# In the first tile, a step's second layer is issued behind the next step's first layer, and the planner's durations are replaced

## The chip, the cores and the metric

The kernel runs on one core of a Trainium2 chip. Its time is the device time of one execution in microseconds (us). Three runs of the kernel before took 511.29, 515.15 and 515.39 us (median 515.15). One more execution was profiled; it took 513.02 us and is the one that the trace describes.

The engines are named as the profile names them: PE (matrix multiply; PEld is its weight load), DVE (vector), ACT (activation functions and copies), POOL (GpSimd) and SP, which here only issues the DMA transfers. Each engine takes its instructions in the order in which they were written, so an instruction that waits holds up everything behind it on its engine.

## The reference

A linear recurrence over 768 positions for each of 4 x 8 heads, and on its 3072 x 384 output a two-layer network with a GELU between:

```python
for t in range(S):                                  # S = 768, D = 48
    cur = einsum('bhd,bhe->bhde', u * k[t], v[t])
    y[t] = einsum('bhd,bhde->bhe', r[t], state + cur)
    state = w * state + einsum('bhd,bhe->bhde', k[t], v[t])
h = x @ w_in                                        # 3072x384 @ 384x2048
g = 0.5 * h * (1.0 + erf(h / sqrt(2)))
return g @ w_out                                    # 3072x2048 @ 2048x384
```

## The kernel before

**The work.** The 768 positions are cut into 6 chunks of 128; with 4 batches, a chunk is a *tile* of 512 tokens for the network. In each chunk the heads are handled as four *groups* (pairs of heads and their time halves): decays are multiplied into the transposed inputs (`T`, `Tb`, line 374) and the keys (`N`, `Nb`, line 380); `scores`, `own`, `gains`, `old`, `new` and `gaps` (lines 402 to 447) are PE products; `keep` (lines 478 and 479) copies a group's output from PSUM (`Y`) into the network's input `xx`, a rounded high part on ACT and the remainder on DVE; every group goes through the one `Y`.

**The network.** A tile has 16 *steps*, one for each 128 hidden units; 6 tiles make 96 steps, `m` = 0 to 95. Every product of 32-bit numbers is three products of rounded parts: high x high, low weight x high, high weight x low. Step m's *first layer* is `product1` (line 553): 9 matmuls of 128 x 512 into the single PSUM bank `Hp`. ACT then applies the GELU twice (`gh`, line 581, the rounded result; `gf`, line 582, the full one) and DVE forms the remainder `gl` (line 583). Step m's *second layer* is `product2` (line 594): 3 matmuls with `gh` and the high weight, 3 with `gh` and the low one, 3 with `gl`, into three banks `O`. `gh` and `gl` are double buffered.

**The weights** come from HBM as 64-bit floats, 768 KB a step, into one of three buffers `raw` (line 316). They are split once, during the first tile, into `wh` and `wl`, which stay in SBUF: per step, ACT runs lines 329 (`wa`), 331 (`wb`) and 339 (`wh`), and DVE runs 333, 335, 337 and 341 (`wl`). A new transfer into a `raw` buffer needs line 331 and 335 of the step that used it; a new `wa` needs line 341 of the step three before.

**What sets the order.** Nothing is written out by hand. `Plan.add` collects every operation with its engine, a duration in ns, a due time, and the names it reads and writes. `Plan.run` plays this list through: it keeps a clock for each engine, always takes the operation that can start first, and between several that are ready the one with the earliest due time (passed back from its users through the durations); the instructions are issued in the order so found. A transfer's end is worked out with a bus of 360 bytes per ns. While PE would idle before the first layer of step 0, `Plan.run` puts in extra matmuls on zeros (`heat`, the "filler"). So a changed duration changes no instruction, but it can change the order on every engine, the number of these fillers, and nothing else.

**Opening.** The loads of the first four groups, two later groups and the first weights are issued in the order of `LOADS` (line 40); `in_turn` lets only three be under way, through a small POOL copy (line 214) that reads a landed buffer and writes a word of the next one. `first_group` handles the four groups of chunk 0; the last three of them are the input that step 0 needs. Here the four are called group 1 to 4, in the order in which they run.

Of the kernel before, what the change touches and what calls it, by code (L numbers as in the profile page):

```python
# [13 lines left out]
AF = mybir.ActivationFunctionType  # L14
# [4 lines left out]
B, H, S, D = 4, 8, 768, 48  # L19
# [7 lines left out]
NJ = DF // 128  # L27
# [5 lines left out]
WMIN, WMAX = 0.7, 1.25  # L33
NT = 8
NEAR = 8
LATER = 10 ** 7
FIRST, STEP, STEP_LAST = 23000, 8400, 3900
WEIGHT_AHEAD, GROUP_AHEAD, GROUP_DUE = 12500, 28000, 20000
# [6 lines left out]
class Plan:  # L45
# [9 lines left out]
    def add(self, eng, ns, at, fn, r=(), w=()):  # L55
        n = len(self.ops)
        deps = set()
        for x in r:
            deps.add(self.writer.get(x))
            self.readers.setdefault(x, []).append(n)  # L60
        for x in w:
            deps.add(self.writer.get(x))
            deps.update(self.readers.pop(x, ()))
            self.writer[x] = n
        deps -= {None, n}
        self.ops.append((eng, ns, at, fn, deps))
        self.reads.append(set(r))
# [3 lines left out]

    def time(self, n):
        e, ns = self.ops[n][:2]
        return 2200 + ns / 360.0 if e == "sp" else ns

    def lag(self, n, m):
        e = self.ops[n][0]
# [4 lines left out]
    def run(self):  # L82
        left = [len(o[4]) for o in self.ops]
        users = [[] for _ in self.ops]
        due = [o[2] for o in self.ops]
        for n in reversed(range(len(self.ops))):
            for d in self.ops[n][4]:
                users[d].append(n)
                due[d] = min(due[d], due[n] - self.time(d) - self.lag(d, n))
        ready_at = [0.0] * len(self.ops)  # L90
        pools = {e: [] for e in self.LAG}
        free = {e: 650.0 for e in self.LAG}
        bus, clear, unread = 0.0, 0.0, 0
        for n, k in enumerate(left):
            if not k:
                pools[self.ops[n][0]].append(n)
        for _ in self.ops:
            best = None
            for e, pool in pools.items():
                if not pool:  # L100
                    continue
                start = max(free[e], min(ready_at[n] for n in pool))
                n = min((n for n in pool if ready_at[n] <= start), key=lambda n: (due[n], n))
                if best is None or start < best[0]:
                    best = (start, e, n)
            start, e, n = best
            if e == "pe" and self.filler:
                fill, buf, ns, room = self.filler
                while not unread and not self.hold and max(free[e], clear) + room < start:
                    fill()  # L110
                    free[e] = max(free[e], clear) + ns
            pools[e].remove(n)
            _, ns, _, fn, _ = self.ops[n]
            if e == "sp":
                free[e] = start + 640
                bus = max(bus, start + 1050) + ns / 360.0
                end = bus + 940
            else:
                free[e] = end = start + ns
            fn()  # L120
            if self.filler:
                unread += sum(self.filler[1] in self.reads[m] for m in users[n] if self.ops[n][0] == "pe")
                if self.filler[1] in self.reads[n]:
                    unread -= 1
                    clear = end + self.LAG[e]
            for m in users[n]:
                ready_at[m] = max(ready_at[m], end + self.lag(n, m))
                left[m] -= 1
                if not left[m]:
                    pools[self.ops[m][0]].append(m)  # L130


def rwkv_gelu_mlp(tc, rkT, rkv, wuT, uN, wmlp, r, k, vT, w, u, out):
    nc = tc.nc
    with ExitStack() as ctx:
# [18 lines left out]
        O = []  # L154
# [4 lines left out]
        wh = [sb([128, 2, DM], F32R, f"wh{j}", cst) for j in range(NEAR)]  # L159
        wl = [sb([128, 2, DM], F32R, f"wl{j}", cst) for j in range(NEAR)]  # L160
# [33 lines left out]
        act = lambda n: 95 + n / 1.2  # L194
        sdve = lambda n: 145 + n / 0.96
        sdve2 = lambda n: 145 + n / 1.92
        sact = lambda n: 225 + n / 1.2
        pool = lambda n: 110 + n * 2.15

        flat2 = lambda x: x.rearrange("p a b c -> p (a b c)")  # L200
# [349 lines left out]
        def product1(x, j, n, ks=range(3), start=False, stop=False):  # L550
            wt, a = ((wh, 0), (wl, 0), (wh, 1))[n]
            for k_ in ks:
                nc.tensor.matmul(O[3], lhsT=wt[j][:, 0, k_ * 128:(k_ + 1) * 128], rhs=x[:, a, k_, :],  # L553
                                 start=start and k_ == ks[0], stop=stop and k_ == ks[-1])
# [8 lines left out]
        def moe1(m, at):  # L563
            t, j = divmod(m, NJ)
            high, low, GH, GL = hidden(m)
            x, X = xx[t % 2], f"xx{t % 2}"

            xr = lambda a, ks=range(3): [f"{X}{k_}{a}" for k_ in ks]
            gaps = [f"{X}{k_}g{i}" for k_ in range(3) for i in range(2)]
            n1 = 2 * j  # L570
            if m == 0:
                gaps0 = lambda k_: gaps[2 * k_:2 * k_ + 2]
                for k_ in range(3):
                    add("pe", 3 * 216, at + k_, lambda k_=k_: [setattr(plan, "filler", None)] + [
                        product1(x, j, n, (k_,), k_ == 0 and n == 0, k_ == 2 and n == 2) for n in range(3)],
                        r=["wh0", "wl0"] + xr("h", (k_,)) + xr("l", (k_,)) + gaps0(k_), w=["H"])
            else:
                for n in range(3):
                    add("pe", 3 * 216, at + n, lambda n=n: product1(x, j, n, start=n == 0, stop=n == 2),
                        r=[f"{('wh', 'wl', 'wh')[n]}{n1}"] + xr("hhl"[n]) + gaps, w=["H"])  # L580
            add("act", 480, LATER, lambda: nc.scalar.activation(out=high, in_=O[3], func=AF.Gelu), r=["H"], w=[GH])  # L581
            add("act", 480, LATER, lambda: nc.scalar.activation(out=gf, in_=O[3], func=AF.Gelu), r=["H"], w=["gf"])  # L582
            add("dve", dve(512), LATER, lambda: nc.vector.tensor_tensor(  # L583
                out=low, in0=gf, in1=high.bitcast(F32), op=ALU.subtract), r=["gf", GH], w=[GL])


# [4 lines left out]
        def product2(j, high, low, n, part):  # L591
            wt, gt = ((wh, high), (wl, high), (wh, low))[n]
            d, dst, a, b = part
            nc.tensor.matmul(bank(dst)[:, a:b], lhsT=wt[j][:, 1, d * 128:(d + 1) * 128], rhs=gt[:, a:b],  # L594
                             start=(j == 0 and n == 0), stop=(j == NJ - 1 and n == 2))

        def moe2(m, at, dest):
# [4 lines left out]
            def go(m, n, which, at):  # L602
                j = m % NJ
                high, low, GH, GL = hidden(m)
                add("pe", 216 * len(which), at, lambda: [product2(j, high, low, n, parts[i]) for i in which],
                    r=[f"{('wh', 'wl', 'wh')[n]}{2 * j + 1}", (GH, GH, GL)[n]], w=[banks[i] for i in which])


            if m < NSTEP - 2:
# [234 lines left out]
```

## Time and profile before

| what | value |
|---|---|
| three runs | 511.29, 515.15, 515.39 us |
| the profiled execution | 513.02 us |
| its span, first to last instruction | 511.2 us |
| PE busy | 484.0 us (95% of the span) |
| DVE, ACT, POOL busy | 242.8, 205.6, 72.2 us |
| granted TensorE clock, mean over the span | 0.975 |
| bytes moved | 43.85 MB, mean 86 GB/s |

The span is read from the first instruction; all times below are from there. A row of the time line has the start in us, the length in us, the engine, the line of the kernel, the operation, `out<-in` by the program's names, the shapes and the count; the bracket gives how long the engine had stood idle and what it waited for. A row of the windows has a stretch of time and in it each engine's busy time (and count), the granted clock of the matrix engine as a fraction, the share of time for which the DMA engines were busy, and GB/s. In the stream of instructions matmuls overlap: three of 128 x 512 take 0.70 us from start to start, though each is shown with about 0.4 us.

### The profile page before, as it was taken

To read this page: it belongs to the slowest core of one execution; us is meant where nothing else is said; L and a number is where in the kernel's file an instruction comes from. 1 tells how busy PE (TensorE), PEld (TensorE's weight loads), DVE (VectorE), ACT (ScalarE), POOL (GpSimd) and SP (SyncE) were. 2 spreads that over 40 slices of the span, in tenths; PEclk is the share of its full clock that TensorE was granted. 3 is DMA by queue.
4 is the path that set the end of the run, shared out by engine and by line. 5 is a ranking of instruction groups with operands and counts; after the bars stand their busy time and mean duration, and the time that the engine had idled before them with its cause. 6 is when DMAs were issued, how large, how long until landed. Compare 5 with 4: busy or idle time off the path is not lost.

```text
span 511.2 us, 11447 instructions
## 1 busy us (share of the span) xinstructions
PE 484.0 (95%) x5006; PEld 387.4 (76%) x5006; DVE 242.8 (47%) x366; ACT 205.6 (40%) x435; POOL 72.2 (14%) x80
## 2 busy tenths in 40 slices
PE   6949998899999999999999999999999999999995
PEld 4846776667787787787787788787787787888884
DVE  5769899899524253724254254253243231211111
ACT  3447567574543433442432432432432422322221
POOL 4310001030220221310220220220220200000000
PEclk9578999999999999999999999999999999999999
DMA  7864528443303033403033123033123000100001
GB/s 221 248 207 170 173 90 263 131 149 94 115 33 94 1 94 94 146 0 94 1 95 93 63 85 92 3 94 93 63 83 92 2 13 10 63 0 1 0 1 66
DMA packets 13190, 43.85 MB, mean 86 GB/s; under 512 B 1808, under 2 KB 2192, under 8 KB 13136
## 3 DMA queue, kind: packets, MB, share of 16 engines
q1 hardware_dynamic: 13136, 43.07, 27.4%
q8 instruction: 41, 0.67, 0.5%
q14 instruction: 13, 0.11, 0.1%
HBM read 36.38 MB, written 4.72 MB: 80 GB/s over the span
## 4 chain that ended last, share of the span: by engine, by line
PE 84%; DMA 9%; DVE 2%; ACT 2%; issue 2%; POOL 1%; SPq 0%; ACTq 0%; POOLq 0%
PE Hp L553 37%; PE O L594 37%; DMA raw<-in_wmlp_dram 7%; PE Y L436 3%; PE Y L426 3%; PE A L407 2%; DMA N<-in_rkv_dram 2%; PE Y L418 1%; PE Y L594 1%; ACT gh L581 1%; DVE wl L341 0%; ACT wh L339 0%; DVE gl L583 0%; ACT wa L329 0%; DVE wa L337 0%
## 5 line engine op out<-in xcount | busy, mean ns | idle before, releaser
L553 PE MATMUL Hp<-xx,wh 128*128 128x512 f32 x576 | 167.6, 399 | 1.4 <-ACT wh L339 1.4
L583 DVE TENSOR_TENSOR gl<-gf,gh 128x512 fp32r<-128x512 f32 x95 | 70.6, 743 | 188.9 <-ACT gf L582 188.8
L581 ACT ACTIVATE gh<-Hp 128x512 fp32r<-128x512 f32 x95 | 56.8, 598 | 232.8 <-PE Hp L553 232.8
L553 PEld LDWEIGHTS Hp<-xx,wh 128*128 128x128 f32 x576 | 107.7, 190 | 26.6 <-ACT wh L339 2.0
L594 PE MATMUL O<-gh,wh 128*128 128x512 f32 (+1 forms) x285 | 83.4, 399 | 5.4 <-ACT gh L581 5.3
L553 PE MATMUL Hp<-xx,wl 128*128 128x512 f32 x288 | 84.4, 400 | 0.2 <-DVE wl L341 0.2
L594 PE MATMUL O<-gl,wh 128*128 128x512 f32 (+1 forms) x285 | 80.8, 390 | 0.1
L594 PE MATMUL O<-gh,wl 128*128 128x512 f32 (+1 forms) x285 | 80.7, 390 | 0.0
L594 PEld LDWEIGHTS O<-gh,wh 128*128 128x128 f32 x285 | 51.6, 188 | 21.9 <-ACT gh L581 10.1
L553 PEld LDWEIGHTS Hp<-xx,wl 128*128 128x128 f32 x288 | 54.3, 189 | 14.0 <-DVE wl L341 1.0
L594 PEld LDWEIGHTS O<-gl,wh 128*128 128x128 f32 x285 | 52.5, 188 | 12.2 <-DVE gl L583 0.6
L594 PEld LDWEIGHTS O<-gh,wl 128*128 128x128 f32 x285 | 52.5, 188 | 11.6
L582 ACT ACTIVATE gf<-Hp 128x512 f32<-128x512 f32 x96 | 56.9, 592 | 0.0
L378 POOL TENSOR_TENSOR Nb<-Nb 128x384 f32<-128x384 f32 x16 | 18.4, 1150 | 256.7 <-DMA Nb<-in_rkv_dram 218.4
L398 ACT ACTIVATE Am<-diag,cs 128x64 f32<-128x64 f32 x128 | 33.5, 344 | 6.3 <-DVE cs L393 6.2
L380 POOL TENSOR_TENSOR Nb<-Nb,WN 128x384 f32<-128x384 f32 x20 | 27.1, 1354 | 51.2 <-DMA Nb<-in_rkv_dram 49.9
L374 DVE TENSOR_TENSOR Tb<-Tb,E 112x1024 f32<-112x1024 f32 x20 | 25.5, 1275 | 5.1 <-DMA Tb<-in_rkT_dram 4.3
L459 DVE SCALAR_TENSOR_TENSOR Sb<-Sa,E,Y 48x192 f32<-48x192 f32 x40 | 16.5, 413 | 14.5 <-ACT xx L478 9.1
L393 DVE TENSOR_REDUCE cs<-Nb 128x8 f32<-128x384 f32 x16 | 8.8, 551 | 28.5 <-POOL Nb L390 28.5
L329 ACT ACTIVATE wa<-raw 128x768 f32<-128x768 f32 x16 | 14.6, 912 | 15.1 <-DMA raw<-in_wmlp_dram 10.2
L478 ACT CAST xx<-Y 112x512 fp32r<-112x512 f32 (+1 forms) x18 | 10.6, 587 | 24.0 <-PE Y L418 19.4
L341 DVE TENSOR_TENSOR wl<-wa,wh 128x768 fp32r<-128x768 f32 x16 | 16.3, 1020 | 2.0 <-ACT wh L339 1.8
(122 smaller groups left out, 393.3 us busy)
## 6 DMA issues: line engine op xcount, KB each, us to landing
raw<-in_wmlp_dram SPq DMA_DIRECT2D x16, 768.0 KB, 4.8
Nb<-in_rkv_dram SPq DMA_DIRECT2D x16, 576.0 KB, 5.4
Tb<-in_rkT_dram SPq DMA_DIRECT2D x20, 448.0 KB, 3.8
out_dram<-raw SPq DMA_DIRECT2D x5, 768.0 KB, 3.6
xx<-x SPq DMA_DIRECT2D x30, 64.0 KB, 3.0
T<-in_rkT_dram SPq DMA_DIRECT2D x4, 448.0 KB, 5.7
N<-in_rkv_dram SPq DMA_DIRECT2D x4, 384.0 KB, 4.7
Nb<-in_rkv_dram SPq DMA_DIRECT2D x4, 384.0 KB, 6.5
```

What stands on the lines that cost most here:

```text
L341: add("dve", sdve(n), LATER, lambda: nc.vector.tensor_tensor(out=both(wl), in0=af, in1=both(wh).bitcast(F32), op=ALU.subtract), r=[A_, f"w ...
L374: add("dve", sdve(1024), LATER, lambda: nc.vector.tensor_tensor(out=flat, in0=flat, in1=E[:, 0, g.p].rearrange("l h i -> l (h i)").unsquee ...
L378: add("pool", pool(DM), LATER, lambda: nc.gpsimd.tensor_tensor(out=g.n[:, 0], in0=g.n[:, 0], in1=g.n[:, 1], op=ALU.mult), r=[g.K], w=[g.R])
L380: add("pool", pool(DM), LATER, lambda: nc.gpsimd.tensor_tensor(out=g.kn, in0=g.kn, in1=WN[:, g.p].rearrange("s j d -> s (j d)").unsqueeze( ...
L398: add("act", sact(HALF) + 60, LATER, lambda x=x, b=b: nc.scalar.activation(out=g.am[:, x, b, :], in_=diag2, func=AF.Copy, scale=g.sums[:, ...
L426: nc.tensor.matmul(g.y[quarter(j), h, b * HALF:(b + 1) * HALF], lhsT=g.s[h][l, b, :], rhs=g.t[l, 0, b, times(h)], start=(b == 0 and not sp ...
L459: add("dve", 420, at, lambda l=l, x=x, more=more: nc.vector.scalar_tensor_tensor(out=g.s[h + 1][quarter(1 - x)], in0=g.s[h][l], scalar=E[l ...
L553: nc.tensor.matmul(O[3], lhsT=wt[j][:, 0, k_ * 128:(k_ + 1) * 128], rhs=x[:, a, k_, :], start=start and k_ == ks[0], stop=stop and k_ == k ...
L581: add("act", 480, LATER, lambda: nc.scalar.activation(out=high, in_=O[3], func=AF.Gelu), r=["H"], w=[GH])
L582: add("act", 480, LATER, lambda: nc.scalar.activation(out=gf, in_=O[3], func=AF.Gelu), r=["H"], w=["gf"])
L583: add("dve", dve(512), LATER, lambda: nc.vector.tensor_tensor(out=low, in0=gf, in1=high.bitcast(F32), op=ALU.subtract), r=["gf", GH], w=[GL])
L594: nc.tensor.matmul(bank(dst)[:, a:b], lhsT=wt[j][:, 1, d * 128:(d + 1) * 128], rhs=gt[:, a:b], start=(j == 0 and n == 0), stop=(j == NJ - ...
```

## The change

Two things. First, every first-layer operation of step m also writes a name `first{m}`, and in steps 0 to 15 (`m < NJ`, the first tile) every second-layer operation of step m also reads `first{m+1}`. The planner therefore places all of step m's second layer behind all of step m+1's first layer. No instruction is added by that: the name stands for no buffer. Second, numbers in the plan are others: the bus goes from 360 to 270 bytes per ns, a matmul from 216 to 234 ns, a GELU from 480 to 600 ns, `gl` from 598 to 678 ns, the splitting and copying operations of ACT by 25 ns more.

```diff
+RATE = 270.0
-        return 2200 + ns / 360.0 if e == "sp" else ns
+        return 2200 + ns / RATE if e == "sp" else ns
-                bus = max(bus, start + 1050) + ns / 360.0
+                bus = max(bus, start + 1050) + ns / RATE
-        sact = lambda n: 225 + n / 1.2
+        sact = lambda n: 250 + n / 1.2
+            first = [f"first{m}"]
-                    add("pe", 3 * 216, at + n, lambda n=n: product1(x, j, n, start=n == 0, stop=n == 2),
-                        r=[f"{('wh', 'wl', 'wh')[n]}{n1}"] + xr("hhl"[n]) + gaps, w=["H"])
-            add("act", 480, LATER, lambda: nc.scalar.activation(out=high, in_=O[3], func=AF.Gelu), r=["H"], w=[GH])
+                    add("pe", 3 * 234, at + n, lambda n=n: product1(x, j, n, start=n == 0, stop=n == 2),
+                        r=[f"{('wh', 'wl', 'wh')[n]}{n1}"] + xr("hhl"[n]) + gaps, w=["H"] + first)
+            add("act", 600, LATER, lambda: nc.scalar.activation(out=high, in_=O[3], func=AF.Gelu), r=["H"], w=[GH])
...
-            add("dve", dve(512), LATER, lambda: nc.vector.tensor_tensor(
+            add("dve", sdve(512), LATER, lambda: nc.vector.tensor_tensor(
...
-                add("pe", 216 * len(which), at, lambda: [product2(j, high, low, n, parts[i]) for i in which],
-                    r=[f"{('wh', 'wl', 'wh')[n]}{2 * j + 1}", (GH, GH, GL)[n]], w=[banks[i] for i in which])
+
+                next_ = [f"first{m + 1}"] if m < NJ else []
+                add("pe", 234 * len(which), at, lambda: [product2(j, high, low, n, parts[i]) for i in which],
+                    r=next_ + [f"{('wh', 'wl', 'wh')[n]}{2 * j + 1}", (GH, GH, GL)[n]], w=[banks[i] for i in which])
```

What it does to the order is shown at three places. **PE in the first tile, around step 5**, before (`wh4` and `wl4` are step 4's weights, `gh0` and `gl0` its hidden values, `gh1` those of step 5):

```order
L553 MATMUL Hp_593<-xx0_120,wh4_79 128x512 x3
L594 MATMUL O0_590<-gl1_126,wh3_78 128x512
L594 MATMUL O1_591<-gl1_126,wh3_78 128x512
L594 MATMUL O2_592<-gl1_126,wh3_78 128x512
L594 MATMUL O0_590<-gh0_123,wh4_79 128x512
L594 MATMUL O1_591<-gh0_123,wh4_79 128x512
L594 MATMUL O2_592<-gh0_123,wh4_79 128x512
L553 MATMUL Hp_593<-xx0_120,wh5_80 128x512 x3
L553 MATMUL Hp_593<-xx0_120,wl5_88 128x512 x3
L553 MATMUL Hp_593<-xx0_120,wh5_80 128x512 x3
L594 MATMUL O0_590<-gh0_123,wl4_87 128x512
```

and after:

```order
L596 MATMUL O0_563<-gl1_126,wh3_78 128x512
L596 MATMUL O1_564<-gl1_126,wh3_78 128x512
L596 MATMUL O2_565<-gl1_126,wh3_78 128x512
L554 MATMUL Hp_566<-xx0_120,wh5_80 128x512 x3
L554 MATMUL Hp_566<-xx0_120,wl5_88 128x512 x3
L554 MATMUL Hp_566<-xx0_120,wh5_80 128x512 x3
L596 MATMUL O0_563<-gh0_123,wh4_79 128x512
L596 MATMUL O1_564<-gh0_123,wh4_79 128x512
L596 MATMUL O2_565<-gh0_123,wh4_79 128x512
L596 MATMUL O0_563<-gh0_123,wl4_87 128x512
```

Before, three matmuls of step 4's second layer stood ahead of step 5's first layer; now all nine stand behind it, and all nine of step 3's second layer lie between the first layers of steps 4 and 5. In the later tiles PE's order is the old one, but for a few groups' products that stand one or two steps earlier or later.

**ACT in the opening**, from the read of `raw1` (step 1's weights) on; `KB1` are group 4's factors, `xx0` are the copies of groups 2, 3 and 4 out of `Y`, `raw2` and the `raw0` behind it the weights of steps 2 and 3. Before:

```order
L329 ACTIVATE wa1_132<-raw1_129 128x768
L386 ACTIVATE KB1_109<-T3_105,uw_100 112x4x64
L478 CAST xx0_120<-Y_68 128x2x4x64
L386 ACTIVATE KB1_109<-T3_105,uw_100 112x4x64
L456 COPY Sb_97<-UE_73 48x192 x2
L331 ACTIVATE wb1_135<-raw1_129 128x768
L329 ACTIVATE wa2_133<-raw2_130 128x768
L478 CAST xx0_120<-Y_68 128x2x4x64
L456 COPY Sb_97<-UE_73 48x192 x2
L478 CAST xx0_120<-Y_68 128x2x4x64
L339 CAST wh0_75<-wa0_131 128x768
```

After:

```order
L330 ACTIVATE wa1_132<-raw1_129 128x768
L332 ACTIVATE wb1_135<-raw1_129 128x768
L479 CAST xx0_120<-Y_68 128x2x4x64
L457 COPY Sb_97<-UE_73 48x192 x2
L340 CAST wh0_75<-wa0_131 128x768
L330 ACTIVATE wa0_131<-raw0_128 128x768
L479 CAST xx0_120<-Y_68 128x2x4x64
L330 ACTIVATE wa2_133<-raw2_130 128x768
L332 ACTIVATE wb0_134<-raw2_130 128x768
L387 ACTIVATE KB0_108<-Tb0_106,uw_100 112x4x64 x2
L340 CAST wh1_76<-wa1_132 128x768
L583 ACTIVATE gh0_123<-Hp_566 128x512
```

The read of `raw2`, which stood ahead of group 3's copy, now stands behind group 4's; `wh0` has moved ahead of group 4's copy, and so has the read of step 3's weights. The first copy into `xx0` and the two `KB1` now stand ahead of the read of `raw1`.

**SP in the opening**, before:

```order
L221 DMA Tb0_106<-in_rkT_dram 112x1024
L224 DMA Nb0_114<-in_rkv_dram 128x768
L316 DMA raw2_130<-in_wmlp_dram 128x1536
L221 DMA Tb1_107<-in_rkT_dram 112x1024
L224 DMA Nb1_115<-in_rkv_dram 128x768
L709 DMA u_sb_91<-in_uN_dram 64x384 x2
L316 DMA raw0_128<-in_wmlp_dram 128x1536
```

and after:

```order
L222 DMA Tb0_106<-in_rkT_dram 112x1024
L225 DMA Nb0_114<-in_rkv_dram 128x768
L317 DMA raw0_128<-in_wmlp_dram 128x1536
L317 DMA raw2_130<-in_wmlp_dram 128x1536
L222 DMA Tb1_107<-in_rkT_dram 112x1024
L225 DMA Nb1_115<-in_rkv_dram 128x768
L713 DMA u_sb_91<-in_uN_dram 64x384
```

The weights of step 3 (the second use of `raw0`) are now issued ahead of those of step 2. At the very start SP issues `T0` ahead of the small table of decays `wu_sb`, which was first before. On POOL one small copy that lets group 3's `N2` be issued now stands ahead of the multiplication of `N0`. PE runs four filler matmuls instead of one ahead of the transpose of the decays (line 305). DVE forms `wl0` ahead of group 4's remainder instead of behind it, and interleaves its work in the first tile differently by one or two instructions at some twenty places.

More of the change, by code (lines that the diff above doesn't have):

```diff
@@ L573, in moe1 @@
                 for k_ in range(3):
-                    add("pe", 3 * 216, at + k_, lambda k_=k_: [setattr(plan, "filler", None)] + [
+                    add("pe", 3 * 234, at + k_, lambda k_=k_: [setattr(plan, "filler", None)] + [
                         product1(x, j, n, (k_,), k_ == 0 and n == 0, k_ == 2 and n == 2) for n in range(3)],
-                        r=["wh0", "wl0"] + xr("h", (k_,)) + xr("l", (k_,)) + gaps0(k_), w=["H"])
+                        r=["wh0", "wl0"] + xr("h", (k_,)) + xr("l", (k_,)) + gaps0(k_), w=["H"] + first)
             else:
                 for n in range(3):
-                    add("pe", 3 * 216, at + n, lambda n=n: product1(x, j, n, start=n == 0, stop=n == 2),
-                        r=[f"{('wh', 'wl', 'wh')[n]}{n1}"] + xr("hhl"[n]) + gaps, w=["H"])
-            add("act", 480, LATER, lambda: nc.scalar.activation(out=high, in_=O[3], func=AF.Gelu), r=["H"], w=[GH])
-            add("act", 480, LATER, lambda: nc.scalar.activation(out=gf, in_=O[3], func=AF.Gelu), r=["H"], w=["gf"])
-            add("dve", dve(512), LATER, lambda: nc.vector.tensor_tensor(
+                    add("pe", 3 * 234, at + n, lambda n=n: product1(x, j, n, start=n == 0, stop=n == 2),
+                        r=[f"{('wh', 'wl', 'wh')[n]}{n1}"] + xr("hhl"[n]) + gaps, w=["H"] + first)
+            add("act", 600, LATER, lambda: nc.scalar.activation(out=high, in_=O[3], func=AF.Gelu), r=["H"], w=[GH])
+            add("act", 600, LATER, lambda: nc.scalar.activation(out=gf, in_=O[3], func=AF.Gelu), r=["H"], w=["gf"])
+            add("dve", sdve(512), LATER, lambda: nc.vector.tensor_tensor(
                 out=low, in0=gf, in1=high.bitcast(F32), op=ALU.subtract), r=["gf", GH], w=[GL])
```

## The prediction

> **What bounds the kernel now.** I read the page's slices first, then the windows, cut at the turns of the program.
>
> ```profile
> PE   6949998899999999999999999999999999999995
> PEclk9578999999999999999999999999999999999999
> ```
> ```profile
> 29.10:33.40 4.30, 0.01 (x2) 0.00 (x0) 1.27 (x3) 2.10 (x4) 0.56 (x3) 0.85 0.47 122
> 33.40:38.28 4.88, 3.35 (x53) 2.70 (x53) 3.96 (x7) 1.37 (x3) 0.80 (x1) 0.50 0.72 208
> 50.70:125.80 75.10, 69.56 (x849) 52.92 (x848) 68.72 (x96) 47.75 (x77) 6.43 (x5) 1.00 0.47 153
> 132.80:511.20 378.40, 370.59 (x3402) 299.78 (x3401) 132.51 (x204) 130.69 (x307) 49.99 (x42) 1.00 0.19 57
> ```
>
> The first number behind the length is PE's busy time, the third DVE's, then ACT's and POOL's; the third from the end is the granted clock. From 132.8 us on PE is busy 370.6 of 378.4 us, DVE a third of that: there matmuls alone bound the kernel, none is added or taken away, and their order is nearly the old one. What the change does, it does ahead of that, in two stages. In the opening (to 38.3 us, the first matmul of step 0) PE waits. In the first tile PE and DVE are both at nine tenths: DVE is busy 68.7 of 75.1 us, because it splits the weights beside its other work.
>
> The opening's largest gap, in the chain of waits (start, length, what) and in the time lines of ACT and PE:
>
> ```profile
> 23.91 7.20 DMA raw<-in_wmlp_dram
> ...
> 32.04 0.59 ACT xx L478
> ...
> 32.66 0.70 DVE xx L479
> ...
> 33.41 1.22 PE Y L446 x4
> ...
> 35.74 1.15 PE Y L436 x32
> ...
> 39.27 3.55 PE Hp L553 x8
> ```
> ```profile
> 26.59 0.90 ACT L331 ACTIVATE wb<-raw 128x768 int32<-128x768 uint32 x1
> 31.13 0.89 ACT L329 ACTIVATE wa<-raw 128x768 f32<-128x768 f32 x1 [3.64 <-DMA raw<-in_wmlp_dram]
> ```
> ```profile
> 26.67 0.75 PE L446 MATMUL Y<-x,spread 112*128 112x256 f32 x4
> ...
> 28.09 0.67 PE L436 MATMUL Y<-Am,N 64*48 64x64 f32 x32
> ```
>
> Group 3's output was ready at 28.09 + 0.67 = 28.76, but its copy began at 32.04: ACT stood at `wa2`, waiting for step 2's weights, with the copy queued behind it. PE idled 4.3 us, the granted clock fell to 0.50, and group 4's products then took 36.89 - 33.41 = 3.5 us where group 3's took 28.76 - 26.67 = 2.1.
>
> **Part 1, the opening.** In the new order `wa2` stands behind both copies. Group 3's copy can start at 28.8 (`wb1` ends at 27.5), 3.25 us earlier, so group 4's products start at 33.41 - 3.25 = 30.15. PE's gap shrinks to about one us, so I take the higher clock to stay: 2.1 us, output ready at 32.25 instead of 36.89.
>
> What is late next is a new wait: group 4's copy stands behind the read of step 3's weights (`raw0`), a transfer that is now issued ahead of step 2's, once line 335 of step 0 has freed the buffer. That operation (0.95 us) now follows this one of line 333 at once:
>
> ```profile
> 21.81 0.55 DVE L333 TENSOR_SCALAR wa<-wa 128x768 int32<-128x768 int32 x1
> ```
>
> So `raw0` is issued at 21.81 + 0.55 + 0.95 = 23.3, nearly when `raw2` was (23.91); with `raw2`'s 7.2 us it lands at 30.5. Longer is possible, since more is under way; the longest landing of such a transfer in the chain is
>
> ```profile
> 100.38 10.45 DMA raw<-in_wmlp_dram
> ```
>
> and would make it 33.75. I take 31. The read (0.9) ends at 31.9, ahead of the output at 32.25; the copy's remainder on DVE, behind `wl0` and three operations more, is done by about 34.5, and step 0's first layer ends at 35 instead of 39.27 + 3.55 = 42.8.
>
> Next `raw2` is late: 786 KB more ahead of it cost 2.8 us at the 280 GB/s of a full queue,
>
> ```profile
> 10.00:20.00 10.00, 8.29 (x243) 7.49 (x244) 7.35 (x11) 5.27 (x11) 5.12 (x9) 0.58 0.94 280
> ```
>
> so it lands at 31.1 + 2.8 = 33.9. Behind it on ACT stand `wa2`, `wb0`, two `KB0`, `wh1` and two GELUs of step 0 that free the bank. From start to start such operations take
>
> ```profile
> 44.62 0.91 ACT L329 ACTIVATE wa<-raw 128x768 f32<-128x768 f32 x1
> 45.41 0.91 ACT L386 ACTIVATE KB<-Tb,uw 112x256 f32<-112x256 f32 x2
> 46.60 0.60 ACT L581 ACTIVATE gh<-Hp 128x512 fp32r<-128x512 f32 x1 [0.28 <-PE Hp L553]
> 47.09 0.59 ACT L582 ACTIVATE gf<-Hp 128x512 f32<-128x512 f32 x1
> 47.57 0.83 ACT L339 CAST wh<-wa 128x768 fp32r<-128x768 f32 x1
> 48.29 0.94 ACT L331 ACTIVATE wb<-raw 128x768 int32<-128x768 uint32 x1
> ```
>
> 0.8 (`wa`, and so I take `wb` and the pair of `KB`), 0.7 (`wh`) and 1.1 (both GELUs): 4.2 us. Step 1's first layer starts at 38.1 and ends, with 2.1 us for nine matmuls, at 40.2. In the chain of before:
>
> ```profile
> 44.46 2.10 PE Hp L553 x9
> 46.56 1.40 PE O L594 x6
> 47.96 1.09 PE A L407 x64
> 49.05 0.36 PE Y L418 x32
> ```
>
> it ended at 46.56, with three matmuls of second layer done (0.7), but without group 5's products (1.09 + 0.36 = 1.45), which the new order has ahead. Like for like the lead is 46.56 + 1.45 - 0.7 - 40.2 = 7.1. Up to `wl2`, with which the window of 50.7 begins, DVE has seven operations of 0.4 to 0.9 us that wait for nothing else late; I take **6.5 us** there.
>
> Bounds: if both transfers take 10.45 us (3 us more than I took) and the clock halves again (1.4 us more for group 4), the lead is about 2.5; if both land in `raw2`'s 7.2, it is 8.5.
>
> Smaller edits. The table `wu_sb` is issued behind `T0`:
>
> ```profile
> 2.69 0.17 DVE L282 TENSOR_SCALAR E<-wu_sb 112x8 f32<-112x8 f32 x1 [0.39 <-DMA wu_sb<-in_wuT_dram]
> 5.88 0.17 POOL L214 COPY N<-T 1x1 f32<-1x1 f32 x1 [3.11 <-DMA T<-in_rkT_dram]
> 9.03 2.00 DVE L374 TENSOR_TENSOR T<-T,E 112x1024 f32<-112x1024 f32 x1 [1.63 <-POOL T L214]
> 13.37 0.92 ACT L329 ACTIVATE wa<-raw 128x768 f32<-128x768 f32 x1 [1.40 <-DMA raw<-in_wmlp_dram]
> ```
>
> At worst it lands with `T0`, at 5.88 less the half us by which `T0` is issued earlier, and the decays come 2.7 us later. DVE idled 1.63 us ahead of `T1`, and ACT then 1.40 for step 0's weights: this cover takes up all but 0.8 us (without it, 2.7). At best it costs nothing, which I take. [...] Three more fillers (0.23 us each) cost 0.4 at most, or nothing if the decays are late. POOL's earlier copy issues `N2` about 1 us sooner, into a full queue; I count nothing.
>
> **Part 2, the first tile.** Waits of the stretch from 50.7 to 132.8, and DVE's group of the split weights:
>
> ```profile
> PE O L594 <- ACT gh L581: 4.6, 8, 0.7
> DVE gl L583 <- ACT gf L582: 1.4, 3, 0.8
> ```
> ```profile
> L341 DVE TENSOR_TENSOR wl<-wa,wh 128x768 fp32r<-128x768 f32 x13 | 13.5, 1036 | 1.9 <-ACT wh L339 1.8
> ```
>
> Eight times PE waits for the GELU of the step whose first layer it has just done. In the new order nine matmuls of the step before (2.1 us) lie there, and the two GELUs need 1.1: these 4.6 us go. What is late next is `wl`: PE can't use a weight that isn't split, and DVE has 68.7 us of work in 75.1. So the tile gains what DVE gains: at least nothing, at most its 6.4 idle us. The waits for a late GELU, or for a cast queued behind one (1.4 + 1.8 = 3.2), should mostly go: I take **3 us**.
>
> Against it: step 15's first layer now needs `wl15` one second layer earlier.
>
> ```profile
> 124.83 0.96 DVE L341 TENSOR_TENSOR wl<-wa,wh 128x768 fp32r<-128x768 f32 x1
> ```
> ```profile
> 131.96 0.87 PE L594 MATMUL O<-gl,wh 128*128 128x512 f32 x3
> ```
>
> Before, 132.8 - 125.8 = 7.0 us passed from `wl15` to the end of step 15's second layer. Now six matmuls of step 15 come, step 14's second layer, step 16's first, step 15's second: 1.4 + 3 x 2.1 = 7.7. With DVE the bound, that costs **0.7 us**.
>
> **Sum.** -6.5 - 3 + 0.7 = -8.8 us. The profiled execution took 513.02 (1.8 outside its span); 513.0 - 8.8 = 504.2, that is 504. The three runs lie from 511.3 to 515.4 around the profiled one, so I forecast against it, not against the median 515.15, with 2 us each way for that scatter.
>
> **Rivals.**
> *The tile is full on both engines* (0.25): DVE's waits nearly all go and the opening gives 8: 8 + 6 - 0.7 = 13.3, 500 us. For it: with the rows' durations few operations of the new order wait long. Against: the present order lost 6.4 us on DVE.
> *The clock falls again* (0.10): PE waits from 35 to 38.1 for `raw2` and ACT. In the windows, 0.85 on average over 4.3 us means that the clock halved 3.0 us after PE fell idle, at 32.1, and came back only at about 42. Steps 1 and 2 then lose 2.1 to 4 us: 506 to 508. [...]
> *The opening's gain is eaten* (0.15): both transfers take 10.45 us; ACT's blocked copy has only changed its place. 2.5 + 0 to 2 - 0.7 leaves 1.8 to 3.8: 509 to 511, within 1%.
> *A ring of waits, slower* (0.05): `wl` of step m lets its first layer run (1.4), then two GELUs (1.1), `wh` of m+1 behind them on ACT (0.75), `wl` of m+1 (0.9); with the second layers queued behind, PE can't fill the time. That is 4.2 us against DVE's 68.7 / 13 = 5.3 a step, so it doesn't bind; it decides once it exceeds 5.3, as it may where a group's products (1.45 and more) lie in it. The largest wait for `wh` is
>
> ```profile
> 62.50 1.43 DVE L341 TENSOR_TENSOR wl<-wa,wh 128x768 fp32r<-128x768 f32 x1 [0.84 <-ACT wh L339]
> ```
>
> If each of 14 steps paid 0.84, 11.8 - 1.8 = 10 us are added; with the opening's low end -2.5 + 10 + 0.7 = +8, 521 us.
>
> **How the numbers follow.** The forecast has the other 0.45. A measurement can't tell less than about 1% (5 us) from no change. Faster by more: forecast, fuller tile, fallen clock, 0.80; within: 0.15; slower: 0.05. The range goes from the fuller tile less scatter, 498.5, to the eaten gain, 510.5.
>
> **What would show it.** PE's 4.3 us idle ahead of group 4 gone; step 0's first layer beginning near 32 instead of 38; the windows of 32 to 42 at clock 1.00; hardly any wait of PE for `gh` ahead of 130, some for `wl` instead; the last split weight near 117 instead of 125.8, and all behind it shifted as a whole. Wrong, if ACT waits for `raw` again ahead of a copy into `xx`, or if DVE's idle time in the tile grows.

## The result and the profile after

| kernel | runs (us) | median | profiled execution | its span, clock |
|---|---|---|---|---|
| before | 511.29, 515.15, 515.39 | 515.15 | 513.02 | 511.2, 0.975 |
| changed | 506.47, 507.28, 509.41 | 507.28 | 509.41 | 507.7, 0.971 |

The ratio is 0.9898 with a 95% interval of 0.986 to 0.9937: faster, by 1.0%. (The medians in the table lie 7.9 us apart, but two of the three runs before lie at the upper end of its longer series.) Nine runs of the changed kernel beside 28 of the one before, in another session (`e4_changed_again` below), gave medians of 507.83 and 512.55, ratio 0.9915 [0.9881, 0.9948]. So the change is worth some 4.5 to 5 us, where 8.8 were forecast. That 507.28 lies in the range of 498.5 to 510.5 says little: the range holds gains from 2.5 to 14.5 us.

The slices of the changed kernel's page (40 equal slices, busy tenths of PE, and the clock that it was granted):

```profile
PE   7879899999999999999999999999999999999995
PEclk9568999999999999999999999999999999999999
```

And its windows, cut where those of before were cut (PE busy, PEld, DVE, ACT, POOL; the third number from the end is the clock, then DMA share and GB/s):

```profile
29.10:33.40 4.30, 2.28 (x50) 1.77 (x53) 1.49 (x3) 0.00 (x0) 0.35 (x2) 0.72 0.70 203
33.40:38.28 4.88, 4.00 (x93) 3.40 (x85) 3.88 (x6) 2.86 (x5) 1.00 (x1) 0.50 0.07 23
50.70:125.80 75.10, 71.05 (x858) 54.94 (x851) 72.11 (x99) 48.24 (x80) 11.70 (x8) 1.00 0.50 162
132.80:507.00 374.20, 366.42 (x3384) 296.17 (x3382) 130.95 (x201) 126.04 (x294) 48.86 (x42) 1.00 0.18 55
```

The tile looks as forecast: from 50.7 to 125.8 us DVE is busy 72.1 us instead of 68.7. The opening does not. PE was to start group 4's products at 30.15 us, at the full clock; just there it stands idle for 2.8 us, and then it works at half clock until past 38.4 us. PE's time line shows what happened (start, length, line, count; in the bracket the idle time ahead and what ended it):

```profile
15.51 1.08 PE L437 MATMUL Y<-Am,N 64*48 64x64 f32 x26
17.47 0.35 PE L437 MATMUL Y<-Am,N 64*48 64x64 f32 x3 [0.89 <-issue]
...
22.91 0.43 PE L408 MATMUL A<-T,KB 48*64 48x64 f32 x4
24.20 1.01 PE L408 MATMUL A<-T,KB 48*64 48x64 f32 x27 [0.86 <-issue]
...
27.62 0.62 PE L447 MATMUL Y<-x,spread 112*128 112x256 f32 x3
31.03 0.37 PE L447 MATMUL Y<-x,spread 112*128 112x256 f32 x1 [2.79 <-issue]
...
35.04 1.22 PE L447 MATMUL Y<-x,spread 112*128 112x256 f32 x4 [0.79 <-DVE xx L480]
...
38.41 0.79 PE L554 MATMUL Hp<-xx,wh 128*128 128x512 f32 x1
```

Three times PE stands within a group of like products, 26, 4 and 3 matmuls into it, and "issue" says that it waited for nothing that the profile shows. At 31.03 that is the last of the four matmuls of group 3's line 447. Such an idle time is called a *stand* below. Group 4's products (35.04) wait only 0.8 us where they waited 4.3 before, but they begin 1.6 us later than before. ACT's copies show the same:

```profile
26.60 0.92 ACT L330 ACTIVATE wa<-raw 128x768 f32<-128x768 f32 x1
27.43 0.89 ACT L332 ACTIVATE wb<-raw 128x768 int32<-128x768 uint32 x1
33.68 0.59 ACT L479 CAST xx<-Y 128x512 fp32r<-128x512 f32 x1 [5.36 <-PE Y L437]
```

ACT waits for no landing of weights here; it waits 5.4 us for PE.

The waits of PE in the tile (50.7 to 132.8 us; total in us, how many, the longest) and DVE's group of the split weights, after:

```profile
PE Hp L554 <- DVE wl L342: 1.4, 4, 0.7
PE Hp L554 <- ACT gf L584: 1.0, 1, 1.0
PE Hp L554 <- ACT wh L340: 0.7, 1, 0.7
```
```profile
L342 DVE TENSOR_TENSOR wl<-wa,wh 128x768 fp32r<-128x768 f32 x13 | 13.7, 1052 | 1.2 <-ACT wh L340 1.1
```

The wait of `O` for `gh` (4.6 us, 8 times) is gone; 3.1 us of waits ahead of the first layer have come. The last split weights, and the chain behind the last of them:

```profile
47.92 0.93 DVE L342 TENSOR_TENSOR wl<-wa,wh 128x768 fp32r<-128x768 f32 x1
...
119.64 0.96 DVE L342 TENSOR_TENSOR wl<-wa,wh 128x768 fp32r<-128x768 f32 x1
```
```profile
120.65 1.67 PE Hp L554 x6
122.32 2.11 PE O L596 x9
124.43 2.10 PE Hp L554 x9
126.53 2.11 PE O L596 x9
128.63 2.10 PE Hp L554 x9
```

`wl2` (the first row) ends at 48.85 instead of 50.7, `wl15` at 120.6 instead of 125.8, and step 15's second layer, at 128.6, 8.0 us behind `wl15` instead of 7.0.

### The profile page after: what moved, and what is told of

Same layout as the page of the kernel before. It is cut to its first block, busy times and chain, and to the rows that moved or that the text cites. A ratio compares the mean times of both kernels' runs of the same rounds, so it can differ in the third digit from the quotient of the medians.

```text
span 507.7 us, 11458 instructions
## 1 busy us (share of the span) xinstructions
PE 486.0 (96%) x5009; PEld 390.1 (77%) x5009; DVE 243.0 (48%) x366; ACT 205.5 (40%) x435; POOL 71.6 (14%) x80
## 4 chain that ended last, share of the span: by engine, by line
PE 80%; DVE 11%; issue 3%; DMA 3%; ACT 1%; POOL 0%; SPq 0%; DVEq 0%; ACTq 0%; POOLq 0%
PE Hp L554 35%; PE O L596 34%; PE Y L437 3%; PE A L408 3%; PE Y L427 2%; DVE wa L338 2%; DVE wl L342 2%; DVE wa L336 1%; DMA raw<-in_wmlp_dram 1%; PE Y L419 1%; PE Y L596 1%; DVE Am L465 1%; DMA Nb<-in_rkv_dram 1%; DVE gl L585 1%; DVE Tb L375 1%
## 5 line engine op out<-in xcount | busy, mean ns | idle before, releaser
L596 PE MATMUL O<-gh,wh 128*128 128x512 f32 (+1 forms) x285 | 82.2, 395 | 0.2 <-issue 0.2
L391 POOL TENSOR_TENSOR Nb<-Nb,u_sb 128x384 f32<-128x384 f32 x16 | 17.7, 1107 | 0.1
```

The source lines that it names most:

```text
L391: add("pool", pool(DM), LATER, lambda: nc.gpsimd.tensor_tensor(out=g.n[:, 0], in0=g.n[:, 0], in1=u_sb[:, g.p, :].unsqueeze(1).to_broadcast ...
```

## The experiments

There are ten runs, two of them of the unaltered kernels. Two questions led them: which part of the change carries the gain, and why the opening gave so little. The first four shared 28 runs of before (median 512.55), the next four 23 (512.73), the last two 17 (511.76).

**The rule alone.** The kernel before with `first{m}` and `next_` added, all durations as they were:

```diff
+ first = [f"first{m}"]          # written by step m's first layer
+ next_ = [f"first{m + 1}"] if m < NJ else []   # read by step m's second layer
```

> The edit of the second layer's place alone, with all durations of the plan as before; the order of the opening is then that of before on every engine. Theory: the change's gain is the first tile's (step 0's first matmul came at 38.4 us in the changed kernel, at 38.3 before; the end of step 15's second layer at 128.6 against 132.8). So this kernel should give most of it: 3 to 4 us under before, step 0 at 38.3, hardly any wait of PE for gh in the first tile. Rival (the gain comes from the new durations, the look-ahead only moves PE's waits from gh to wl): within 1 us of before, with waits of PE for wl of about the 4.6 us that the waits for gh had.

Measured: 511.22 (10 runs), ratio 0.9974 [0.9946, 1.0002]: 1.3 us, not to be told from nothing. The theory that the rule gives most of the gain fell. Its trace does show the forecast mechanism in the tile. Waits of 50.7 to 132.8 us, where the `gh` wait was the largest:

```profile
DVE gl L585 <- ACT gf L584: 4.9, 4, 2.3
PE Hp L554 <- DVE wl L342: 2.5, 4, 1.6
```

No wait of `O` for `gh` is left, and from `wl2` to `wl15` 71.5 us pass instead of 75.1. But 8.0 us lie between `wl15` and the end of step 15's second layer, and this profiled execution (509.45) was the lowest of the ten. Step 0 began at 36.2 us, not at the 38.3 expected.

**All durations, without the rule.**

```diff
- next_ = [f"first{m + 1}"] if m < NJ else []
+ next_ = []
```

> The new durations alone; a step's second layer may again come ahead of the next step's first. The order of the opening is that of the changed kernel. Theory (the tile's gain is the look-ahead's, the opening's order costs as much as it saves): within 1.5 us of before, step 0 at about 38.4, PE's stalls without a named cause in the opening as in the changed kernel (0.9, 0.9 and 2.8 us). Rival (the durations bring the gain): 3 to 4 us under before.

Measured: 507.52 (9 runs), ratio 0.9904 [0.9864, 0.9943]. The rival won: without the rule the whole gain is there, and with it (`e4_changed_again`) no more. `O` still waits for `gh` 3.7 us here. The opening was not as expected either. Its trace has none of the changed kernel's three stands, and in its chain of waits group 4's products begin at 30.20 us, where the prediction had them; the one stand (2.0 us) comes after that:

```profile
30.20 0.73 PE Y L447 x4
30.93 0.58 PE Y L427 x16
...
32.24 1.99 issue
34.24 0.46 PE Y L437 x6
```

Step 0 began at 34.6 us instead of 38.4.

**Step 3's weights later.** In the changed kernel's plan the transfer into `raw0` for step 3 is placed behind the landing of step 2's (in the trace it is issued at 26.7 us, 3 us behind step 2's, instead of just ahead of it):

```diff
- w=[f"raw{j % 3}"])
+ r=["raw2"] if j == 3 else [], w=[f"raw{j % 3}"])
```

> The changed kernel, with the transfer of step 3's weights issued behind those of step 2 and of the second later group, as before the change; nothing else is edited, so the copy of group 3 is still ahead of the read of step 2's weights, but that read now stands ahead of group 4's copy. Theory (PE ran out of instructions: the 16 KB of instructions that it needed at 24.2 us were moved from 28.55 on, behind 768 KB of weights that the change had put into the queue, and PE stood 2.8 us until 31.0): the instructions are moved at about 24.3 to 25, the stall of 2.8 us falls below 1, group 3's copy begins near 29 to 30 instead of 33.7, step 0's first matmul near 33 to 35 instead of 38.4, and the time is 3 to 5 us under that of the changed kernel. Rival (the decays, 2.4 us late behind T0, or something else in the opening hold it up): the stall stays above 2 us, and step 0 begins at 37 to 39; within 1 us of the changed kernel.

Measured: 509.81 (9 runs), ratio 0.9945 [0.991, 0.9981]. PE's stand inside group 3's line 447 shrank as expected and group 3's copy began at 30.0 us, yet step 0 began only at 36.3 us; a stand of 1.1 us came at the next multiple, record 1217, in group 4's line 437, which has none in the changed kernel:

```profile
25.60 1.01 PE L447 MATMUL Y<-x,spread 112*128 112x256 f32 x3
27.38 0.37 PE L447 MATMUL Y<-x,spread 112*128 112x256 f32 x1 [0.77 <-issue]
...
35.94 0.46 PE L437 MATMUL Y<-Am,N 64*48 64x64 f32 x6 [1.13 <-issue]
```

The time is not 3 to 5 us under the changed kernel's; by the medians it is 2 us above, but the two series overlap almost wholly (505.55 to 512.22, and 505.47 to 511.18). In its one trace, which is near the longest of the nine (511.92), the tile is longer: from step 0's first matmul to the end of 17 first and 16 second layers 94.0 us pass, against 90.2 in the changed kernel, and from `wl2` to `wl15` DVE stands 6.1 us instead of 2.4. So an early transfer may pay back in the tile what it costs in the opening; one trace does not show it.

**The changed kernel again**, for the scatter and for where it stands:

> The changed kernel once more, for a second profile and to set it beside the others on one chip. Theory: PE's stalls of 0.9, 0.9 and 2.8 us at 17.5, 24.2 and 31.0 us stand in this profile too, at the same instructions (every 256th), their lengths different by up to 1 us; step 0 at 37 to 39; 0.5 to 1.5% under before. Rival (the stalls were an accident of one execution): none above 0.5 us, and step 0 begins near 33.

Measured: 507.83 (9 runs), ratio 0.9915 [0.9881, 0.9948]. As the theory had it, the stands are at the same three instructions, 1.25, 1.96 and 3.63 us long. Step 0 begins at 36.2 us, ahead of the 37 to 39 expected.

**The kernel before again**, unaltered:

> The kernel before the change, unaltered, for a second look at its opening. Theory (the 4.3 us that PE stood ahead of group 4's products in the first profile belonged to that one execution, because there step 2's weights landed at 31.1, while the kernel with the same opening order landed them at 27.9 in its look): PE's idle time ahead of group 4 is under 2.5 us here, step 0's first layer starts between 35.5 and 37.5 us instead of 38.3, and something else than the copy stands late. Rival (the idle time is a property of the order, as the prediction took it): 3.5 to 5 us idle there again, behind ACT's wait for the same transfer, and step 0 starts at 38 or later.

Measured: 512.69 (one run). ACT's time line:

```profile
25.23 0.91 ACT L329 ACTIVATE wa<-raw 128x768 f32<-128x768 f32 x1 [4.68 <-DMA raw<-in_wmlp_dram]
26.56 0.58 ACT L478 CAST xx<-Y 128x512 fp32r<-128x512 f32 x1
28.13 0.92 ACT L331 ACTIVATE wb<-raw 128x768 int32<-128x768 uint32 x1
29.63 0.91 ACT L329 ACTIVATE wa<-raw 128x768 f32<-128x768 f32 x1 [0.58 <-DMA raw<-in_wmlp_dram]
32.15 0.58 ACT L478 CAST xx<-Y 128x512 fp32r<-128x512 f32 x1 [1.62 <-PE Y L436]
```

Half of the theory held. The long wait for step 2's weights ahead of group 3's copy, 3.6 us in the first profile, is 0.6 us here, and PE stood 0.8 us ahead of group 4 instead of 4.3. Yet step 0 began at 38.4 us, as the first time: now step 1's weights held up group 2's copy (4.7 us), and the clock stayed at half from 11.5 to 42.2 us. The 4.3 us belonged to one execution; the length of the opening did not hang on them.

**The transfer rate alone.** The kernel before with `ns / 360.0` changed to `ns / 270.0` in its two places, which gives it the changed kernel's opening on SP, ACT and PE and the old tile:

> The kernel before with the transfer rate alone changed (360 to 270 in the two places): it has the changed kernel's opening on SP, ACT and PE (table behind the first transfer, two copies ahead of step 2's read, step 3's transfer ahead of step 2's) and the old durations and rule in the first tile. Prediction's part 1 (the opening is worth 6.5 us): ratio 0.987, about 506 beside 512.5. Theory now (the opening's gain is eaten by step 3's transfer, which delays step 2's weights and PE's instruction blocks): -2 to +1 us, ratio 0.996 to 1.002, step 0 starts at 36 to 38.5.

Measured: 510.73 (12 runs), ratio 0.9965 [0.9936, 0.9994]. The new opening by itself is worth 2.0 us on the clock, not 6.5. In its trace step 0 began at 34.3 us, earlier than expected, and `wl2` ended 4.6 us earlier than before; PE stood at two of the three instructions again (0.7 and 1.8 us).

**All but the rate.** The changed kernel with `RATE = 360.0`:

> The changed kernel with the transfer rate left at 360: the opening is the old one up to the first steps, the tile has the new durations and the new rule. Theory now (the tile alone carries the gain, 2 to 4 us): ratio 0.992 to 0.996, 508.5 to 510.5 beside 512.5; the point at which 17 first layers and 16 second layers are done lies 90 to 92.5 us behind the start of step 0's first layer (94.5 before). Rival (the new opening is needed for it, since the rule alone with this opening gave 1.3 us): ratio 0.997 to 1.001.

Measured: 510.7 (12 runs), ratio 0.9952 [0.9923, 0.9982]: 2.0 us by the medians, at the edge of what was expected. From step 0's first matmul to the end of 17 first and 16 second layers 93.5 us passed, outside the expected 90 to 92.5.

**Instruction blocks shifted.** The stands in the changed kernel lie 256 instructions of PE apart, counted in its trace over matmuls, weight loads and PE's few waits and drains: they come at records 449, 705 and 961. Three of its nine warm-up matmuls give way to 66 short ones, which moves everything behind them by 126 instructions (a part of the edit, with `SHORT` = 3 and `PIECES` = 22):

```diff
+ if n >= HEATS - SHORT:
+     for i in range(PIECES):
+         nc.tensor.matmul(dst[:, 0:64], lhsT=zeros.bitcast(mybir.dt.bfloat16)[:, 0:128],
+                          rhs=zeros.bitcast(mybir.dt.bfloat16)[:, 0:64], start=True, stop=True)
```

> The changed kernel with three of its nine warm-up matmuls replaced by 66 short ones (64 columns) into the same place: 126 more instructions on PE ahead of everything, nothing else moved on any engine. Theory (PE runs out of instructions at the end of each block of 256, because the transfer of the next block waits in the full queue): PE's stalls that wait for nothing the profile shows move by 126 instructions to other lines. In the changed kernel they stood in group 0's products of line 437, in line 408 and at the last matmul of group 4's line 447; here they can stand only at the first pair of keys of line 408 (two places), in line 419 of groups 1 and 3, and not at line 447. Rival (a stall belongs to its place, for a semaphore or the clock): PE stands 2 us or more at the last matmul of line 447 of group 4 again.

(What this text and the next call group 4's line 447 is group 3's by the prediction's count: the matmul at 31.03 above.) Measured: 512.14 (one run), and on PE (this kernel's lines 415, 434 and 454 are the changed one's 408, 427 and 447):

```profile
11.81 0.41 PE L415 MATMUL AE<-T,KB 48*64 48x64 f32 x11
15.36 0.81 PE L415 MATMUL AE<-T,KB 48*64 48x64 f32 x19 [3.14 <-issue]
...
19.90 1.11 PE L415 MATMUL A<-T 48*64 48x64 f32 x26 [0.92 <-DVE T L382]
22.73 0.48 PE L415 MATMUL A<-T 48*64 48x64 f32 x6 [1.72 <-issue]
...
27.86 0.44 PE L415 MATMUL AE<-T 48*64 48x64 f32 x4
32.62 1.01 PE L415 MATMUL AE<-T 48*64 48x64 f32 x27 [4.32 <-issue]
...
34.52 1.22 PE L454 MATMUL Y<-x,spread 112*128 112x256 f32 x4
```

The stands left their lines and came back at other ones, at records 449, 705 and 961 of this trace too; group 3's line 454 runs without a break. The third came in line 415, where 426 (the changed kernel's 419) was expected; in the changed kernel's trace the records of the two lines interleave there. The rest went as the theory said. The three add up to 9.2 us where the changed kernel's two traces had 4.5 and 6.8, and step 0 begins at 42.8.

**A transfer that nobody uses.** The kernel with step 3's weights late, and near their old place in the queue 786 KB into a spare buffer (in the trace 0.4 us behind step 2's weights, where step 3's were 0.4 us ahead of them; a small POOL copy that goes with it is left out here):

```diff
+ if x == "w2":
...
+     dma(128 * 6144, at, lambda: nc.sync.dma_start(spare, wbits[:, 3]), w=["spare"])
```

> The kernel with step 3's weights sent late, and in their old place in the queue a transfer of the same 786 KB into a buffer that nothing uses. Theory (PE's blocks of 256 instructions come late because data is queued ahead of them, whatever it is): at the last matmul of line 447 of group 4, where the kernel with late weights stood 0.8 us, PE stands 1.8 to 4 us again, as in the changed kernel's looks (2.8, 3.6). Rival (the stall hangs on step 3's weights themselves, on ACT's and DVE's work with them): under 1.2 us there.

Measured: 510.73 (one run), and at that matmul

```profile
28.29 0.37 PE L447 MATMUL Y<-x,spread 112*128 112x256 f32 x1 [1.84 <-issue]
```

1.8 us, at the low end of what the theory said and above the rival's bound. It fits that data ahead in the queue lengthens the stand, whatever the data is for. One trace each (0.8 and 1.8) is thin support, and over the whole opening the two differ little: 1.9 us of stands with late weights (the 0.8, and 1.1 in line 437), 2.3 with the spare transfer.

**The durations of PE, ACT and DVE alone**: the kernel before with 234, 250, 600 and `sdve(512)`, but rate 360 and no rule:

> The kernel before with the new durations of PE, ACT and DVE only: transfer rate and rule are the old ones. Theory (the parts add up: rate alone -2.0, rule alone -1.3, all but the rate -2.0): what is left for the engines' durations is -0.5 to -1.5 us, ratio 0.997 to 0.999. Rival (the engines' durations carry most of the 5 us that all durations together gave without the rule): -3 us or more, ratio 0.994 or lower.

Measured: 513.2 (12 runs), ratio 1.0012 [0.9984, 1.004]: nothing, less than either theory had.

**What they make together.** One profiled execution each; "stands" are PE's idle times at records 256 apart, "half clock" the time so granted, both ahead of step 0's first matmul:

| kernel | opening | stands | half clock | step 0 begins | `wl2` ends | `wl15` ends | span |
|---|---|---|---|---|---|---|---|
| before | old | 0 | 19.8 | 38.3 | 50.7 | 125.8 | 511.2 |
| before again | old | 0 | 26.9 | 38.4 | 50.7 | 125.3 | 511.0 |
| rule alone | old | 0.5 | 25.6 | 36.2 | 49.4 | 120.8 | 507.7 |
| all but the rate | old | 1.0 | 18.2 | 35.0 | 45.3 | 120.4 | 508.6 |
| engines' durations | old | 0.5 | 18.2 | 34.8 | 44.8 | 122.9 | 510.6 |
| changed | new | 4.5 | 24.5 | 38.4 | 48.8 | 120.6 | 507.7 |
| changed again | new | 6.8 | 8.4 | 36.2 | 47.5 | 119.1 | 507.8 |
| durations, no rule | new | 2.0 | 12.7 | 34.6 | 46.2 | 119.7 | 505.9 |
| rate alone | new | 2.5 | 13.9 | 34.3 | 46.1 | 121.1 | 507.8 |
| late weights | step 3's later | 1.9 | 19.9 | 36.3 | 46.8 | 122.3 | 510.2 |
| spare transfer | step 3's later | 2.3 | 19.1 | 35.7 | 44.9 | 119.1 | 508.8 |
| blocks shifted | new | 9.2 | 27.5 | 42.8 | 53.3 | 123.6 | 510.4 |

"Old" and "new" are the order of the transfers and of the two copies against step 2's read; with the engines' new durations ACT also casts `wh0` ahead of group 4's copy. Step 0 begins at 36.5 us on average with the old opening (34.8 to 38.4) and at 35.9 with the new one (34.3 to 38.4). These averages leave out the last three rows. The orders differ less than two executions of one kernel. Within the old opening the two kernels with the early `wh0` begin step 0 at 34.9 on average and the three others at 37.6, so that cast may matter as much as the transfers; no run tests it alone. The column of `wl2` is no mark of equal work: DVE's order differs, and PE has by then done 30 to 36 matmuls of the two layers in most rows, but only 22 to 27 with the engines' durations, all but the rate, the late weights and the spare transfer.

## Why the prediction was right or wrong

Span by span, the two traces of before against the two of the changed kernel:

| step | forecast | measured |
|---|---|---|
| the opening, to the end of `wl2` | -6.5 | -1.9 and -3.2 (50.7, 50.7 to 48.8, 47.5) |
| the tile, `wl2` to `wl15` | -3 | -3.4 and -3.0 (75.1, 74.6 to 71.7, 71.6) |
| behind `wl15`, to the end | +0.7 | +1.7 and +3.0 (385.4, 385.7 to 387.1, 388.7) |
| sum | -8.8 | -3.5 and -3.2 |

By the medians the change is worth 4.7 us, somewhat more than these single executions show.

**The step that failed is Part 1**: "Group 3's copy can start at 28.8 [...] so group 4's products start at 30.15", and behind it "I take the higher clock to stay: 2.1 us". In the changed kernel the copy began at 33.68 and the products at 35.04, 4.9 us late. The rows above account for it: group 3's products began 0.95 us later than before, PE stood 2.8 us among them, and the rest of them took 1.1 us longer, at half clock from 31.0 us on. Group 4's products then took 3.4 us, not 2.1. So the opening gave 1.9 and 3.2 us, about the low bound of 2.5 us, instead of the 6.5 taken. Two more kernels have this opening. In the one without the rule group 3's copy began at 28.27 and group 4's products at 30.20, as forecast, and with the rate alone at 29.56 and 30.93; `wl2` ended 4.5 and 4.6 us earlier than before there. So the order can do what Part 1 says, and even then not all of the 6.5 came. Three things were wrong in it.

First, the 4.3 us were one execution's. The second trace of before has 0.8 us there and the other kernels with the old opening 0.8 to 2.0: 1.9 on average over five traces, against 1.0 over four with the new one. The changed order takes away 0.9 there, not 3.25.

Second, "what is late next" was answered with a landing (step 3's weights), which came in time: ACT waited for no landing ahead of either copy. What was late was PE's own instructions: the 16 KB packet of them ahead of the stand's end at 31.03 us was moved from 28.55 on. With 786 KB more queued, PE stood 2.0 to 6.8 us at the ends of its blocks of 256 instructions ahead of step 0, against 0 to 1.0 with the old opening: on average 3.5 us more. The prediction priced each wait that the profile names and had no term for this one, which the profile calls "issue". That these stands come from the instructions is shown by the shifted blocks; that the 786 KB alone make the difference is not, since the stands of the late weights and of the spare transfer add up to nearly the same.

Third, "I take the higher clock to stay". In all four traces with the new opening the clock was 0.50 again from 27.2 to 32.1 us on, through group 4's products or from their middle on, and the time at half clock ahead of step 0 varies from 8 to 27 us between executions. So no one value of it served to cost these orders. Each of the four has stands (2.0 to 6.8 us) beside its half clock (8.4 to 24.5 us), and no run prices the clock by itself.

The smaller edits cost nothing, as taken. The decays came at the late end of the two cases, 2.4 us later than before:

```profile
5.06 0.17 DVE L283 TENSOR_SCALAR E<-wu_sb 112x8 f32<-112x8 f32 x1 [2.75 <-DMA wu_sb<-in_wuT_dram]
```

Yet group 1's line 427 began at 14.24 us, where before it had begun at 14.68.

**Part 2 was right in size, and its mechanism is seen.** The waits for `gh` (4.6 us) are gone in the three traces with the rule that were read for it, and stayed in the three without it (4.8, 4.5 and 3.7); the tile gained 3.2 us of the 3 taken, and DVE's idle time between `wl2` and `wl15` fell from 6.4 to 2.4 us. The rows that replaced the old wait are as forecast: PE now waits for `wl`. But the gain is not the rule's alone. Between marks of equal work (from step 0's first matmul to the end of 17 first and 16 second layers) before takes 94.5 and 94.0 us, the rule alone 92.6, all durations without the rule 92.0, and both together 90.2 and 90.9. And on the clock the rule adds nothing to the durations that the runs can tell (507.83 with it, 507.52 without).

**The price behind `wl15` was too low.** The path was the forecast one, matmul by matmul (six, nine, nine, nine), and took 8.0 us against 7.7 forecast and 7.0 before. All seven traces of kernels with the rule show 8.0 there, the five without it 6.9 to 7.6. From the end of that path, with the same layers done as before, the changed kernel then takes 0.7 and 2.0 us longer to the end than before. A new wait of PE near 204 us stands there, 0.8 us in the first trace and 1.1 in the second:

```profile
PE A L408 <- DVE Tb L375: 0.8, 1, 0.8
```

So +0.7 became +1.7 and +3.0. This is not all the rule's: the kernels without it also take 0.7 to 2.3 us more behind `wl15` than before. The rule alone has +1.5 there (386.9), which takes back part of a tile as short as the whole change's.

**The rivals.** *The opening's gain is eaten* (0.15) was the nearest: 2.5 from the opening, by another mechanism than the one it named. *The clock falls again* (0.10) came true in part: half clock from 31.0 to 41.2 us is there, but its price cannot be told from the rest. *The ring of waits* and *the tile full on both engines* did not happen. Neither of the two signs named for being wrong came: ACT did not wait for `raw` ahead of a copy, and DVE's idle time fell. Step 0's begin ("near 32"), the clock ("1.00" from 32 to 42) and the last split weight ("near 117", measured 120.6 us) were the signs that failed. The range's low end, 498.5, is 1.2 us under the fuller tile's 513.0 - 13.3 = 499.7, not the 2 us of scatter named; nothing hangs on it.

**What stays open.** The parts do not add up by the medians: the rate alone gained 2.0 us, the rule alone 1.3, the engines' durations alone lost 1.4, yet all durations without the rule gained 5.0 and everything 4.7. Each carries an interval of some 1.5 us either way, so part of that may be scatter; that the engines' durations help only with the new opening would fit as well, and no run tells these apart. No kernel tried beats the changed one by more than its interval.

## What to carry to other kernels

Before a gap in one profiled execution is priced, profile a second one: a wait of 4.3 us that came from a landing was 0.8 us the next time, while the stage around it kept its length. When an order puts more data into a queue early, ask what else comes by DMA at that time; here it was the matrix engine's instructions, 16 KB at a time, and the profile called the 2.8 us that the engine stood only "issue". And where a rule removes a wait from the middle of a stage, price its end too: nine matmuls moved behind the last weight cost back 1.0 us of the 3.2 that the tile gained.

## What the runs showed of the hardware

The page of the changed kernel has a DMA queue for instructions, and counts 5009 matmuls and 5009 weight loads on PE:

```profile
PE 486.0 (96%) x5009; PEld 390.1 (77%) x5009; DVE 243.0 (48%) x366; ACT 205.5 (40%) x435; POOL 71.6 (14%) x80
...
q8 instruction: 41, 0.67, 0.6%
```

0.67 MB in 41 packets is 16 KB each, one packet for each 244 of PE's 10 018 matmuls and weight loads. The stands, 0.4 to 4.3 us long, come at records 449, 705, 961 or 1217, so a multiple of 256 instructions apart, though not at each of them in each execution, and they move with the instructions (`e8_blocks_shifted`). So a packet is read here as a block of 256 instructions of PE, and a stand as the wait for the next block. The trace has the packets' times: the last one ahead of the stand's end at 31.03 us was moved from 28.55 to 29.53, though PE had entered the block before it (record 705) at 24.20, 4.35 us earlier. The next but one was moved 0.84 us after PE had entered a block, from 38.80 on, when the data queue was nearly idle (DMA share 0.07 in the window to 38.28). Idle time of 0.6 to 1.6 us near 10 to 11 us, which three profiles also put to "issue", lies at no such record and is not counted. From PE's record 705 to the start of the packet ahead of record 961 the times differ most: 1.4 us in before, 4.35 in the changed kernel, 0.6 in the one without the rule, where PE did not stand there, and 7.2 in the one with shifted blocks, where it stood 4.3; the data packets begun in that time are 0.2, 1.5, 0.1 and 1.9 MB. In these four the packet came the later, the more data was moved meanwhile; a longer time also lets more data pass, so they do not show by themselves which caused which. That less data queued ahead shortens the stand is supported by the spare transfer (0.8 us to 1.8) and by the late weights (2.8 and 3.6 to 0.8), one or two traces each.

The second is the clock. In the second trace of before it was granted 0.50 from 11.5 to 42.2 us without a break, while PE was as busy as this:

```profile
29.10:33.40 4.30, 3.53 (x84) 2.94 (x83) 2.67 (x6) 2.03 (x4) 0.35 (x2) 0.50 0.77 213
```

In the changed kernel's second trace the half clock took only 8.4 us of the time ahead of step 0. The stretches of half clock that begin ahead of step 0 lasted 17.07 and 10.24 us in the changed kernel's first trace, 13.65 and 10.24 in before's first and 30.7 in its second: five, three, four, three and nine times 3.41 us. PE was busy for 3.53 of 4.30 us within the longest. How busy PE has to be for the full clock no run here shows.
